# Two layers of linear attention and a squared-ReLU MLP: turned features stored one round later, and one block's normed rows turned by VectorE and reordered through DRAM

## The chip, the cores and the metric

The kernel runs on one core of a Trainium2 chip. The metric is the device time of one execution, in microseconds (us); lower is better. Three runs of the kernel before took 2440.19, 2440.58 and 2441.8 us, median 2440.58. The engines are named as in the profile: PE is the matrix engine (PEld its weight loads), DVE the vector engine, ACT the scalar engine, POOL the GpSimd engine, and SP the queue that issues nearly all DMAs.

## The reference

The input is 2048 rows of 576 features in fp32. Two layers follow each other with the same weights; a layer is linear attention with a learned softmax feature map (32 heads of 18), then an MLP with 4608 hidden units and a squared ReLU, each on layer-normed rows and added to its input.

```python
def _A_ref(x, wqkv, w_phi, wo):          # linear attention
    q, k, v = ...                        # (x @ wqkv), 32 heads of 18
    pq = einsum("bhsd,hdf->bhsf", q, w_phi);  pk = ... the same of k
    phi_q = concatenate([softmax(pq), softmax(-pq)], axis=-1)
    phi_k = concatenate([softmax(pk), softmax(-pk)], axis=-1)
    kv = einsum("bhsf,bhsd->bhfd", phi_k, v);  z = phi_k summed over s
    o = (phi_q @ kv) / (phi_q @ z + 1e-6)
    return o @ wo
def _B_ref(x, w1, b1, w2, b2):           # MLP
    r = maximum(x @ w1 + b1, 0)
    return (r * r) @ w2 + b2
for _ in range(2):
    x = x + _A_ref(layernorm(x), ...)
    x = x + _B_ref(layernorm(x), ...)
```

## The kernel before

**Tiling.** The 2048 rows are four blocks of 512; a block is four tiles of 128 rows. Every fp32 operand of a product is split into a high part (rounded) and a low part (the rest), and a product is made of high x high, high x low and low x high on PE. A block that goes into an MLP must lie turned in SBUF, with the features on the partitions: tiles `...nh` (high, five chunks of 128 x 512) and `...nl` (low, four chunks; the 64 features that remain share the fifth chunk of the high tile, high below and low above).

**Stages of a layer.** First a barrier stage for the block that opens the layer. Then the MLP of that block (in the trace `m_3` in the first layer, `m_1` in the second; here "the first MLP" of a layer), the MLP of a second block (`m_2`, `m_0`; "the second MLP"), and last a stage for the other two blocks together. While an MLP runs, the attention of other blocks is woven into it. In the first layer the first MLP has beside it the output part of the attention of block 2 (tiles `a_2...`) and the queries and feature maps of block 0 (`a_0...`); the second MLP has the output part of block 0 and all of block 1 (`a_1...`). In the second layer the same stages run with other block numbers. In both layers the first woven block is the one that the second MLP then needs.

**The MLP** (`g_mlp`, L1110) runs over 36 chunks f of 128 hidden units. For each, SP loads w1's columns (L1159, L244) and w2's rows (L1161); ACT copies them into high parts (L1167 to L1169), DVE and POOL make the low parts (L1171, L1174, L1175). `hidden` (L1190) makes 14 matmuls into one PSUM tile `ph` (tag "h", a single buffer): 5 of high x high, 4 with the low rows, and 5 with the low weights. `square` lets ACT take the ReLU into `hr` (L1197), its square into `hb` (L1198) and the unrounded square (L1199), and DVE the low part (L1200). `second` makes 15 matmuls into the accumulators `acc` (L1217 and L1208). In the code `second(f - 1)` stands behind `hidden(f)`, so that ACT has a whole chunk's time for the square.

**Weaving.** `weave` (L104) takes a step of the MLP, adds a rate to an account and draws steps of the other generator while the account covers their cost (the number that each `yield` gives). That sets the order of the program; the instruction order on each engine comes from a scheduler that works on it with its own estimates, within the dependences and the `issue_after` bounds. What is left of the other generator at the end of the first MLP is drawn behind the last rows but one of its output ("rows", L1926).

**What the change touches.** `g_features.turn` (L895) turns a tile of 128 rows x 1152 features in 32 x 32 squares on DVE (L897) and stores it with four DMAs into DRAM (`...ft`), in an order that puts features on rows; `g_out.fetch` (L922, L928) loads it back, features on partitions. All DMAs of SP leave in one order, and an issue that waits for its DVE or DMA holds those behind it. `g_out` ends with eight output products of 28 matmuls each (L999, two halves of 288 columns for each of four tiles), their adds on DVE (L1004) and the norm, `g_norm` (L466): statistics on DVE (L459, L462) and POOL (L463, L464), scaling on DVE (L490 and L495), transposes on PE against an identity (L512, 16 of them; L526, 4), and from PSUM the split by ACT (L520, L533) and DVE (L521, L534). `keep` adds a bias on POOL (L1051) and stores the rows (L1052). In `g_attend` (L1680) the cost of each step of this last part is 3.0 where no other norm is given, and its last steps get a cost of 99.0 there, which leaves them to the drain at the end of the MLP; with a norm given they keep their own costs.

## Time and profile before

| | us |
|---|---|
| median of three runs | 2440.58 |
| the profiled execution | 2441.59 |
| its span in the trace | 2439.9 |
| PE busy | 2410.0 (99%) |
| DVE busy | 1560.5 (64%) |
| ACT busy | 1289.7 (53%) |
| POOL busy | 940.6 (39%) |
| first MLP of the first layer, in the trace | 227 to 501.7 |
| second MLP of the first layer | 501.7 to 798.5 |
| first and second MLP of the second layer | 1434 to 1709, 1709 to 2006 |

The profiled execution stands 1.0 us above the median, and 1.7 us of it lie outside the span. A timeline row gives start, duration, engine, line, operation, tiles and shapes, how many instructions in a row it joins, and in brackets the engine's idle time just before and what released it. Matmuls overlap in their records: the distance from one start to the next is what one costs, and that is shorter than its recorded duration. Tile names are joined over blocks and layers of the same name, so a place is given by its time.

### The profile page before, as it was taken

How to read it: one execution, taken by the hardware profiler on the slowest of the kernel's cores; microseconds unless marked ns; L12 is line 12 of the kernel's file. 1: busy time of each engine (PE TensorE's matmuls, PEld its weight loads, DVE VectorE, ACT ScalarE, POOL GpSimd, SP SyncE). 2: the span in 40 equal slices, each digit the busy share in tenths (PEclk: the TensorE clock that was granted, in tenths of full speed). 3: DMA queues.
4: the chain of work that ended last, by engine and by line, in shares of the span. 5: the costliest groups of instructions: out<-in, count | busy, mean ns of one | idle time of the engine just before them, and what ended most of it. 6: DMA issues, size and time to landing. Idle time of an engine off the chain costs nothing. (4 is left out here: it accounts for less than half of the span.)

```text
span 2439.9 us, 41475 instructions
## 1 busy us (share of the span) xinstructions
PE 2410.0 (99%) x14806; PEld 2137.9 (88%) x14806; DVE 1560.5 (64%) x2537; ACT 1289.7 (53%) x2543; POOL 940.6 (39%) x1121
## 2 busy tenths in 40 slices
PE   9999999999999999999999999999999999999999
PEld 8999888888888888888999988888887888888898
DVE  8779847664867655545766787486557675555443
ACT  4344555444456666664443444554455466676643
POOL 4555303212335565542433442032222455565321
PEclk9999999999999999999999999999999999999999
DMA  9124573666654533338753156537667444333364
GB/s 338 64 84 165 163 194 97 151 202 220 155 173 136 157 99 115 109 104 302 257 188 139 59 173 143 168 96 186 191 233 158 141 142 145 118 103 116 110 199 130
DMA packets 370646, 379.40 MB, mean 155 GB/s; under 512 B 142886, under 2 KB 270790, under 8 KB 367878
## 3 DMA queue, kind: packets, MB, share of 16 engines
q1 hardware_dynamic: 369180, 375.37, 51.2%
q8 instruction: 116, 1.90, 0.3%
q10 hardware_dynamic: 1258, 1.37, 0.2%
q14 instruction: 92, 0.75, 0.1%
HBM read 297.22 MB, written 79.41 MB: 154 GB/s over the span
## 5 line engine op out<-in xcount | busy, mean ns | idle before, releaser
L1507 POOL TENSOR_TENSOR m_ps<-m_pr,m_ps 128x128 fp32r<-128x128 f32 x144 | 98.6, 685 | 337.8 <-ACT m_ps L1505 310.7
L1506 DVE TENSOR_TENSOR m_ps<-m_pr,m_ps 128x448 fp32r<-128x448 f32 x144 | 99.8, 693 | 175.9 <-ACT m_ps L1504 175.8
L1549 PE MATMUL m_pacc<-m_ps,m_phb 128*128 128x448 f32 x864 | 185.6, 363 | 0.0
L1549 PEld LDWEIGHTS m_pacc<-m_ps,m_phb 128*128 128x128 f32 x864 | 161.9, 188 | 15.0
L1549 PE MATMUL m_pacacc<-m_ps,m_phc 128*128 128x448 f32 x648 | 147.1, 365 | 0.0
L1504 ACT ACTIVATE m_ps<-m_pr 128x448 fp32r<-128x448 f32 x144 | 82.8, 575 | 115.7 <-issue 64.9
L1549 PEld LDWEIGHTS m_pacacc<-m_ps,m_phc 128*128 128x128 f32 x648 | 119.2, 188 | 7.7
L1190 PE MATMUL m_0ph<-a_0nh,m_0h 128*128 128x512 f32 (+1 forms) x380 | 96.7, 382 | 1.6 <-ACT m_0hr L1197 1.4
L1190 PE MATMUL m_1ph<-t1onh,m_1h 128*128 128x512 f32 (+1 forms) x380 | 96.2, 381 | 2.0 <-ACT m_1hr L1197 1.8
L1217 PE MATMUL m_2acc<-m_2s,m_2hb 128*128 128x448 f32 x432 | 95.2, 367 | 2.9 <-ACT m_2s L1168 2.6
L1190 PE MATMUL m_3ph<-t0onh,m_3h 128*128 128x512 f32 (+1 forms) x380 | 96.1, 381 | 1.8 <-ACT m_3hr L1197 1.6
L1217 PE MATMUL m_0acc<-m_0s,m_0hb 128*128 128x448 f32 x432 | 95.0, 367 | 2.9 <-ACT m_0s L1168 2.6
L1190 PE MATMUL m_2ph<-a_2nh,m_2h 128*128 128x512 f32 (+1 forms) x380 | 96.6, 382 | 0.8 <-ACT m_2hr L1197 0.6
L1217 PE MATMUL m_3acc<-m_3s,m_3hb 128*128 128x448 f32 x432 | 94.2, 364 | 2.0 <-ACT m_3hb L1198 1.4
L1217 PE MATMUL m_1acc<-m_1s,m_1hb 128*128 128x448 f32 x432 | 94.2, 364 | 2.0 <-ACT m_1hb L1198 1.4
L1217 PEld LDWEIGHTS m_2acc<-m_2s,m_2hb 128*128 128x128 f32 x432 | 81.8, 190 | 11.7 <-ACT m_2s L1168 3.0
L1217 PEld LDWEIGHTS m_0acc<-m_0s,m_0hb 128*128 128x128 f32 x432 | 81.5, 190 | 11.7 <-ACT m_0s L1168 3.0
L1217 PEld LDWEIGHTS m_3acc<-m_3s,m_3hb 128*128 128x128 f32 x432 | 80.4, 188 | 10.6 <-ACT m_3hb L1198 2.1
L1217 PEld LDWEIGHTS m_1acc<-m_1s,m_1hb 128*128 128x128 f32 x432 | 80.4, 188 | 10.5 <-ACT m_1hb L1198 2.1
L1175 POOL TENSOR_TENSOR m_3s<-m_3r,m_3s 128x128 fp32r<-128x128 f32 x36 | 22.9, 637 | 161.9 <-ACT m_3s L1169 153.3
L1175 POOL TENSOR_TENSOR m_1s<-m_1r,m_1s 128x128 fp32r<-128x128 f32 x36 | 22.8, 635 | 162.0 <-ACT m_1s L1169 151.8
L1190 PEld LDWEIGHTS m_1ph<-t1onh,m_1h 128*128 128x128 f32 x380 | 68.8, 188 | 17.4 <-ACT m_1hr L1197 3.0
(2464 smaller groups left out, 7237.0 us busy)
## 6 DMA issues: line engine op xcount, KB each, us to landing
m_pr<-in_B_w SPq DMA_DIRECT2D x144, 288.0 KB
m_pr<-in_B_w SPq DMA_DIRECT2D x72, 256.0 KB
hd<-m_pu SPq DMA_DIRECT2D x72, 256.0 KB
m_pg<-hd SPq DMA_DIRECT2D x72, 256.0 KB
m_3r<-in_B_w SPq DMA_DIRECT2D x36, 288.0 KB
m_2r<-in_B_w SPq DMA_DIRECT2D x36, 288.0 KB
m_1r<-in_B_w SPq DMA_DIRECT2D x36, 288.0 KB
m_0r<-in_B_w SPq DMA_DIRECT2D x36, 288.0 KB
```

What stands on the lines that cost most here:

```text
L1175: nc.gpsimd.tensor_sub(s2[:, FC + P : FC + 2 * P], r2[:, R:], s2[:, FC : FC + P].bitcast(F32))
L1190: dense["hidden"] = nc.tensor.matmul(ph[:, cols], a, m, start=(k == 0), stop=(k == len(ops) - 1))
L1217: nc.tensor.matmul(acc[t][:, :R], a[:, rows], m, start=(f == 0 and k == 0), stop=(f == NF - 1 and k == 2))
L1504: nc.scalar.activation(s2[:, RO : RO + R], r2[:, :R], AF.Copy)
L1506: nc.vector.tensor_sub(s2[:, RO + R : RO + 2 * R], r2[:, :R], s2[:, RO : RO + R].bitcast(F32))
L1507: nc.gpsimd.tensor_sub(s2[:, FC + P : FC + 2 * P], r2[:, R:], s2[:, FC : FC + P].bitcast(F32))
L1549: nc.tensor.matmul(accs[b][t][:, :R], a[:, rows], m, start=(g == 0 and k == 0), stop=(g == NF - 1 and k == 2))
```

## The change

Two things are done differently.

First, the stores of the turned features become a stage of their own in the pipeline of `g_features`: tile t is stored one round after it was turned (while the next tile is worked on), and the last one after a further wait of 4.0 cost units. `g_out` waits 3.0 units after its first two fetches.

Second, the norm of the first woven block of each layer is `g_norm_far` in place of `g_norm`. The rows are scaled by one DVE instruction of 128 x 576, turned in 32 x 32 squares by DVE, and stored by four DMAs per tile into a DRAM tile `...xt`, in the same way as the features. One load then fetches the block with the features on partitions into the low tile, and two loads fetch the last 64 features; ACT makes the high parts (L624) and DVE subtracts (L625), chunk by chunk. The 20 transposes of that block on PE fall away. Since a norm is now given, the last steps of `g_out` have their own costs, and are not left to the drain. The rates of the two weaves go from 3.7 to 4.4 and from 5.0 to 5.1.

```diff
@@ -584,6 +584,56 @@
                 apart(NT - 1)
                 yield 1.6
 
+    def blocks_out(home, flat, t):
+        for i in range(NQ):
+            at = t * P + 32 * i
+            nc.sync.dma_start(home[:, at : at + 32].rearrange("(j f) r -> f j r", f=32),
+                              flat[32 * i : 32 * i + 32].rearrange("f (j r) -> f j r", r=32))
+
+    def g_norm_far(x_of, dst, name, then=None):
+        home = dram.tile([D, TB], F32, name=f"{name}xt")
+        xns, raw = {}, {}
+
+        def rows(t):
+            x = x_of(t)
+            mv, rstd = moments(x, t, name)
+            xns[t] = sb.tile([P, D], F32, tag="qk", name=f"{name}n{t}", bufs=5)
+            nc.vector.tensor_scalar(xns[t], x, mv[:, 0:1], rstd, op0=ALU.subtract, op1=ALU.mult)
+            if then:
+                then(t, x)
+
+        def turn(t):
+            nc.vector.transpose(xns[t], xns[t])
+
+        def store(t):
+            blocks_out(home, xns.pop(t), t)
+
+        def land():
+            dst.update(xt_tiles(name))
+            nc.sync.dma_start(dst["l"].bitcast(F32), home[: KC * P].rearrange("(c p) n -> p c n", p=P))
+            raw["t"] = sb.tile([P, TB], F32, tag="ft", name=f"{name}t", bufs=4)
+            load_twice(raw["t"], home, 0, TB)
+
+        def split(c):
+            if c < KC:
+                hi, src, p = dst["h"][:, c], dst["l"][:, c].bitcast(F32), slice(0, P)
+                lo = dst["l"][:, c]
+            else:
+                hi, src, p = dst["h"][:, c], raw["t"], slice(DT, P)
+                lo = dst["h"][DT:, c]
+            nc.scalar.activation(hi, src, AF.Copy)
+            dense["normed"] = nc.vector.tensor_sub(lo, src[p], hi[p].bitcast(F32))
+
+        yield from pipeline(NT, (rows, turn, lambda t: t < NT - 1 and store(t)), (3.0, 0.9, 0.2))
+        yield 3.0
+        store(NT - 1)
+        yield 3.0
+        land()
+        yield 4.0
+        for c in range(NC):
+            split(c)
+            yield 0.8
+
     def spill(b, x):
         nc.sync.dma_start(xth[b], x["h"].rearrange("p c n -> p (c n)").bitcast(F32))
         nc.sync.dma_start(xtl[b], x["l"].rearrange("p c n -> p (c n)").bitcast(F32))
@@ -895,13 +945,18 @@
         def turn(t):
             flat = ph[t].rearrange("p s d -> p (s d)")
             nc.vector.transpose(flat, flat)
-            for i in range(NQ):
-                at = t * P + 32 * i
-                nc.sync.dma_start(home[:, at : at + 32].rearrange("(j f) r -> f j r", f=32),
-                                  flat[32 * i : 32 * i + 32].rearrange("f (j r) -> f j r", r=32))
-
-        yield from held(pipeline(NT, (start, lambda t: soft_exp(ph[t]), add, factors, lambda t: phi_scale(ph[t], rs[t]),
-                                      turn), (2.6, 0.4, 3.0, 2.8, 1.2, 1.6)), ("last", "squared"))
+
+        def store(t):
+            blocks_out(home, ph[t].rearrange("p s d -> p (s d)"), t)
+
+        def steps():
+            yield from pipeline(NT, (start, lambda t: soft_exp(ph[t]), add, factors, lambda t: phi_scale(ph[t], rs[t]),
+                                     turn, lambda t: t < NT - 1 and store(t)), (2.6, 0.4, 3.0, 2.8, 1.2, 1.6, 0.2))
+            yield 4.0
+            store(NT - 1)
+            yield 0.2
+
+        yield from held(steps(), ("last", "squared"))
 
     def g_out(layer, b, ph, dst, name, parts=1, pause=None, behind=None, norm=None, mid=None, costs=(None, None), o_first=None):
 
@@ -1013,6 +1068,7 @@
         if parts == 1:
             for k in range(2):
                 fetch(k)
+            yield 3.0
         xs_of = []
         if pause:
             product, total, factors, rescale = pause
@@ -1839,7 +1895,7 @@
         def back_first():
             m, later = f"a{layer}_{order[2]}", []
             mid = (g_queries(layer, order[2], None, later, m), g_features(layer, later, early, m))
-            yield from g_attend(layer, order[1], None, raws, nxt, f"a{layer}_{order[1]}", dense, None, mid)
+            yield from g_attend(layer, order[1], None, raws, nxt, f"a{layer}_{order[1]}", dense, g_norm_far, mid)
 
         def back_second():
             yield from g_attend(layer, order[2], None, None, operands, f"a{layer}_{order[2]}", None,
@@ -1923,14 +1979,14 @@
                 if last:
                     keep.update(x=xk, es=es, v=wpair("v", f"w{m}"))
 
-        weave(g_mlp(layer, order[0], ready, [], f"m{layer}_{order[0]}", dense.pop("rest")), chained(back_first()), 3.7, "rows")
+        weave(g_mlp(layer, order[0], ready, [], f"m{layer}_{order[0]}", dense.pop("rest")), chained(back_first()), 4.4, "rows")
         back = chained(back_second())
 
         def then():
             drain(back)
             next(products)
 
-        weave(g_mlp(layer, order[1], nxt, [], f"m{layer}_{order[1]}", None, then), back, 5.0)
+        weave(g_mlp(layer, order[1], nxt, [], f"m{layer}_{order[1]}", None, then), back, 5.1)
         back = iter(()) if layer else chained(back_keys(), True)
         for k, _ in enumerate(products):
             if k == NP - 1:
```

What moves on the engines is shown at three places, in the first layer; the second layer has the same. Line numbers behind the change are those of the changed kernel (`hidden` is L1246 there, `second` L1273 and L1264, the copies L1223 to L1225, the low parts L1227 and L1230, the square L1253 to L1256, the stores L590).

On PE, near the end of the first MLP, before: `m_3ph` is the hidden product, `m_3acc` the second one; the number in `m_3h_34` or `m_3s_33` is the chunk f.

```order
L1190 MATMUL m_3ph_5827<-t0onh,m_3h_34_5819 128x512 x5
L1190 MATMUL m_3ph_5827<-t0onl,m_3h_34_5819 128x512 x4
L1190 MATMUL m_3ph_5827<-t0onh,m_3h_34_5819 128x512 x5
L1217 MATMUL m_3acc_3539<-m_3s_33_5655,m_3hb_5843 128x448 x2
L1217 MATMUL m_3acc_3540<-m_3s_33_5655,m_3hb_5843 128x448 x2
L1217 MATMUL m_3acc_3541<-m_3s_33_5655,m_3hb_5843 128x448 x2
L1217 MATMUL m_3acc_3542<-m_3s_33_5655,m_3hb_5843 128x448 x2
```

The same place in the changed kernel:

```order
L1246 MATMUL m_3ph_5865<-t0onh,m_3h_34_5857 128x512 x5
L1246 MATMUL m_3ph_5865<-t0onl,m_3h_34_5857 128x512 x4
L1246 MATMUL m_3ph_5865<-t0onh,m_3h_34_5857 128x512 x5
L1273 MATMUL m_3acc_3539<-m_3s_34_5858,m_3hb_5935 128x448 x2
L1273 MATMUL m_3acc_3540<-m_3s_34_5858,m_3hb_5935 128x448 x2
L1273 MATMUL m_3acc_3541<-m_3s_34_5858,m_3hb_5935 128x448 x2
L1273 MATMUL m_3acc_3542<-m_3s_34_5858,m_3hb_5935 128x448 x2
```

Before, the second product of chunk 33 stands behind the hidden product of chunk 34; now it is that of chunk 34 itself. In the whole first MLP the second product stands directly behind the hidden product of its own chunk at f = 13 before, and at f = 11, 12, 31, 32, 33, 34 and 35 in the changed kernel. There the eight output products of the woven block (112 matmuls `a_2po`) stand in one piece between chunks 28 and 29; before, they were spread from chunk 29 to the end.

On DVE, around the output part of the woven block, before (`a_2x` is a tile of its rows, `a_2nn` and `a_2ne` the normed rows, `m_3h_31` the low weights of chunk 31):

```order
L459 BN_STATS a_2ns_5732<-a_2x_5698 128x6
L462 BN_AGGR a_2nm_5733<-a_2ns_5732 128x2
L490 TENSOR_SCALAR a_2nn_5740<-a_2x_5698,a_2nm_5733,a_2nd_5734 128x512
L1174 TENSOR_TENSOR m_3s_30_5436<-m_3r_30_5430,m_3s_30_5436 128x448
L495 TENSOR_SCALAR a_2ne<-a_2x_5698,a_2nm_5733,a_2nd_5734 128x128
L1171 TENSOR_TENSOR m_3h_31_5494<-m_3r_31_5488,m_3h_31_5494 128x640
```

The end of the same part in the changed kernel:

```order
L1059 TENSOR_TENSOR a_2x_5800<-a_2po_5802,a_2x_5800 128x288
L459 BN_STATS a_2ns_5834<-a_2x_5800 128x6
L1059 TENSOR_TENSOR a_2x_5800<-a_2po_5818,a_2x_5800 128x288
L459 BN_STATS a_2ns_5834<-a_2x_5800 128x6
L462 BN_AGGR a_2nm_5835<-a_2ns_5834 128x2
L601 TENSOR_SCALAR a_2nn_5842<-a_2x_5800,a_2nm_5835,a_2nd_5836 128x576
L606 STREAM_TRANSPOSE a_2nn_5842<-a_2nn_5842 128x576
L1227 TENSOR_TENSOR m_3h_29_5402<-m_3r_29_5396,m_3h_29_5402 128x640
```

Before, two tiles' parts stood together, and low weights were made among them; now the 28 instructions of all four tiles stand in one piece, the low weights of chunk 29 behind them.

On SP, in the middle of the second MLP, before (`m_2r_17` is w2's rows of chunk 17, `a_1ft` the DRAM tile of block 1's turned features, `a_1Q1e` the second of its four tiles):

```order
L1159 DMA m_2r_18_7536<-in_B_w 128x4x128
L244 DMA m_2r_18_7536<-in_B_w 64x128 x2
L900 DMA a_1ft<-a_1Q0e 32x36x32 x4
L900 DMA a_1ft<-a_1Q1e 32x36x32 x4
L1161 DMA m_2r_17_7473<-in_B_w 128x576
L900 DMA a_1ft<-a_1Q2e 32x36x32 x4
L1161 DMA m_2r_18_7537<-in_B_w 128x576
```

The same place in the changed kernel:

```order
L1215 DMA m_2r_18_7519<-in_B_w 128x4x128
L244 DMA m_2r_18_7519<-in_B_w 64x128 x2
L590 DMA a_1ft<-a_1Q0e 32x36x32
L1217 DMA m_2r_17_7456<-in_B_w 128x576
L590 DMA a_1ft<-a_1Q0e 32x36x32 x3
L1217 DMA m_2r_18_7520<-in_B_w 128x576
L590 DMA a_1ft<-a_1Q1e 32x36x32 x4
```

The load of w2's rows for chunk 17 stood behind the stores of two tiles, and stands behind one store of the first; that for chunk 18 stood behind three tiles, and stands behind one.

## The prediction

> **What bounds the kernel now.** I read the page's busy line first, then the busy time by stretch (columns: stretch, length, PE, PEld, DVE, ACT, POOL with their counts, clock, DMA share, GB/s), then what PE waits for.
>
> ```profile
> PE 2410.0 (99%) x14806; PEld 2137.9 (88%) x14806; DVE 1560.5 (64%) x2537; ACT 1289.7 (53%) x2543; POOL 940.6 (39%) x1121
> 230.00:501.70 271.70, 267.97 (x1341) 233.24 (x1339) 187.84 (x279) 140.29 (x257) 74.09 (x76) 1.00 0.60 159
> 501.70:798.50 296.80, 292.51 (x1507) 255.72 (x1505) 191.06 (x315) 156.40 (x308) 99.60 (x124) 0.99 0.60 174
> 1437.00:1709.00 272.00, 268.00 (x1340) 233.00 (x1339) 188.84 (x279) 140.25 (x257) 73.89 (x76) 1.00 0.59 159
> 1709.00:2006.00 297.00, 291.47 (x1503) 255.25 (x1501) 189.84 (x313) 155.35 (x305) 97.98 (x123) 0.99 0.60 174
> ```
>
> PE is busy 99% of the span at full clock, and in the four MLP stretches that the change touches it idles 3.7, 4.3, 4.0 and 5.5 us. So the time is PE's instructions plus PE's waits; work on DVE, ACT or SP counts only where PE waits for it. The waits of PE (total us, times, longest), two rows from the first MLP, two from the second, and the second layer's largest:
>
> ```profile
> PE m_3ph L1190 <- ACT m_3hr L1197: 1.6, 2, 0.8
> PE m_3acc L1217 <- ACT m_3hb L1198: 1.4, 1, 1.4
> PE m_2acc L1217 <- ACT m_2s L1168: 2.6, 1, 2.6
> PE m_2ph L1190 <- ACT m_2hr L1197: 0.6, 1, 0.6
> PE m_0acc L1217 <- ACT m_0s L1168: 2.6, 1, 2.6
> ```
>
> The 1.4 in the first MLP is the one chunk (f = 13) whose second product stands directly behind its own hidden product. The 2.6 in the second MLP is a late copy of weights.
>
> **Term 1: second products directly behind their own hidden product.** The changed order has seven of them in each first MLP, the old one has one. The trace shows its price, first that chunk, then an ordinary one:
>
> ```profile
> 317.57 1.29 PE L1190 MATMUL m_3ph<-t0onh,m_3h 128*128 128x512 f32 x5
> 318.91 0.69 ACT L1197 ACTIVATE m_3hr<-m_3ph,b1t 128x512 f32<-128x512 f32 x1 [6.16 <-PE m_3ph L1190]
> 319.62 0.63 ACT L1198 ACTIVATE m_3hb<-m_3hr 128x512 fp32r<-128x512 f32 x1
> 320.31 2.68 PE L1217 MATMUL m_3acc<-m_3s,m_3hb 128*128 128x448 f32 x12 [1.44 <-ACT m_3hb L1198]
> 323.52 1.30 PE L1190 MATMUL m_3ph<-t0onh,m_3h 128*128 128x512 f32 x5
> ...
> 429.98 1.29 PE L1190 MATMUL m_3ph<-t0onh,m_3h 128*128 128x512 f32 x5
> 431.11 2.57 PE L1217 MATMUL m_3acc<-m_3s,m_3hb 128*128 128x448 f32 x12
> 434.22 1.31 PE L1190 MATMUL m_3ph<-t0onh,m_3h 128*128 128x512 f32 x5
> ```
>
> From the last five hidden matmuls to the next chunk's first: 323.52 - 317.57 = 5.95 us in the direct case, 434.22 - 429.98 = 4.24 in the ordinary one. The difference, 1.71 us, is ACT's ReLU and square (0.69 + 0.63) with the handovers, and nothing of PE's lies behind it. Six more: 6 x 1.71 = **+10.3 us** a layer. ACT started 0.05 us after PE's end there, so it can't be less by an idler ACT. If other ACT work stood between, it would be more.
>
> **Term 2: the eight output products in one piece.** Before, the DVE chain of a tile and the parts of the transpose:
>
> ```profile
> 448.66 1.38 DVE L897 STREAM_TRANSPOSE a_0Q3e<-a_0Q3e 128x1152 f32<-128x1152 f32 x1
> 449.96 0.42 DVE L1004 TENSOR_TENSOR a_2x<-a_2po,a_2x 128x288 f32<-128x288 f32 x1
> 452.97 0.55 DVE L490 TENSOR_SCALAR a_2nn<-a_2x,a_2nm,a_2nd 128x512 f32<-128x512 f32 x1 [1.00 <-POOL a_2nd L464]
> 453.69 0.45 DVE L1004 TENSOR_TENSOR a_2x<-a_2po,a_2x 128x288 f32<-128x288 f32 x1
> 458.12 0.81 DVE L1171 TENSOR_TENSOR m_3h<-m_3r,m_3h 128x640 fp32r<-128x640 f32 x1
> ```
>
> A tile takes 453.69 - 449.96 = 3.73 us, with PE's products back to back beside it. In the changed order a tile takes 3.01 us to the scaling (449.96 to 452.97), about 0.62 for 576 columns (scaled from 0.55 for 512) and half of 1.38 for its transpose: 4.3 us, and four of them 17.2, while PE needs 4 x 3.73 = 14.9. The chain starts one product (1.9 us) after PE and ends at 19.1; behind it stands the low part of chunk 29's weights (0.81), at 19.9. PE, which has two PSUM tiles for these products, is held up about 1 us among them, and then gets 2.0 us into chunk 29 (nine matmuls) before it needs those low weights, so it waits 2 to 3 us more: about 4 in all. Of the old order's waits in this place one is a 0.8 for the ReLU, where two hidden products stand together; such a pair stands in both orders and stays. What else can go is what PE's idle time in the stretch (3.7 us) leaves beside the 1.6 and 1.4 of the wait rows: 0.7, with its handovers some 1 us. I take 4 - 1 = **+3.0** a layer, between 0 (if DVE keeps pace with PE) and +4.2 (if none of the old waits go).
>
> **Term 3: the end of the first MLP.**
>
> ```profile
> 500.30 1.14 DVE L1275 TENSOR_TENSOR m_3x<-m_3acc,m_3x 128x448 f32<-128x448 f32 x2
> 501.73 0.84 PE L1190 MATMUL m_2ph<-a_2nh,m_2h 128*128 128x256 f32 x5
> 502.63 0.67 DVE L1277 TENSOR_TENSOR m_3x<-m_3py,m_3x 128x128 f32<-128x128 f32 x3
> 497.56 0.60 ACT L520 ACTIVATE a_2nh<-a_2np 128x512 fp32r<-128x512 f32 x1 [4.84 <-PE a_2np L512]
> ```
>
> In the changed order ACT makes one high part of the landed rows (0.60) between the last chunk's ReLU and its square, which that chunk's direct product waits for: +0.6. DVE's eight adds for the output rows (four of 0.57 and four of 0.22, 3.2 us) and a low part (0.81) now stand ahead of the new MLP's first low weights; PE has four transposes and 16 half-width matmuls at 0.13 or so to do meanwhile, some 2.7 us: +1.1 to +1.3. I take **+1.7** a layer, between 0 and +4.0 (all of DVE's work uncovered).
>
> **Term 4: 20 transposes leave PE.**
>
> ```profile
> L512 PE MATMUL a_2np<-ident,a_2nn 128*128 128x128 f32 x16 | 2.4, 272 | 0.0
> 454.26 0.60 PE L512 MATMUL a_2np<-ident,a_2nn 128*128 128x128 f32 x4
> 455.05 0.40 PE L999 MATMUL a_2po<-a_2o0h,a_2oh 126*128 126x288 f32 x1 [0.18 <-DVE a_2x L1004]
> 496.92 0.60 PE L512 MATMUL a_2np<-ident,a_2nn 128*128 128x128 f32 x4
> 497.28 1.17 PE L1208 MATMUL m_3acc<-m_3hb,m_3s 128*128 128x512 f32 x4
> ```
>
> Each is recorded with 272 ns, but four of them move what follows by 0.36 us (496.92 to 497.28), or 0.61 less the wait (454.26 to 455.05). At 0.4 for four: **-2.0** a layer, between -1.8 and -3.1. [...]
>
> **Term 5: the late weights in the second MLP.**
>
> ```profile
> SPq L900 <- DVE a_1Q1e L897: 7.9, 1, 7.9
> 649.43 2.33 SPq L900 DMA_DIRECT2D a_1ft<-a_1Q1e  x4
> 651.86 0.59 SPq L1161 DMA_DIRECT2D m_2r<-in_B_w  x1
> 655.61 1.29 PE L1190 MATMUL m_2ph<-a_2nh,m_2h 128*128 128x512 f32 x5
> 658.86 0.56 ACT L1168 ACTIVATE m_2s<-m_2r 128x448 fp32r<-128x448 f32 x1
> 664.63 2.57 PE L1217 MATMUL m_2acc<-m_2s,m_2hb 128*128 128x448 f32 x12
> ```
>
> The first row is SP's wait, the others are instructions. w2's rows for chunk 17 leave SP behind the stores of block 1's second tile, which waited 7.9 us for its transpose; ACT's copy of them stands behind chunk 18's ReLU and squares and starts at 658.86. Chunk 17's second product takes from 656.74 (655.61 plus 1.13, as 429.98 to 431.11) to 664.63, 7.89 us where an ordinary one takes 434.22 - 431.11 = 3.11: 4.8 us lost. Changed, that load stands behind one store of the first tile, and the copy ahead of chunk 18's ReLU: the loss goes. Late next is the first load for chunk 19, now behind the third tile's stores, and one more pair of hidden products (chunks 19 and 20) at the 0.8 of the wait rows: together about +1, against about 0.7 of smaller waits that go. I take **-4.5** a layer, between 0 (the stall only moves) and -7.2 (all of PE's waits here go).
>
> **Costed at nothing.** The added stores (16 a layer, of 128-byte runs), the three loads and DVE's four transposes lie beside PE; the DMA share is 0.60 in these stretches. SP has the loads for the block ahead of the end: it issues them behind those of chunk 35's weights, which wait for chunk 33's to be used, some two chunks (2 x 8.0 us) before ACT copies the block. If that cover is gone, each us is a us on PE, since the last square stands behind a copy.
>
> **The sum.** +10.3 + 3.0 + 1.7 - 2.0 - 4.5 = +8.5 a layer, +17.0 for both. Against the profiled execution that is 2441.6 + 17.0 = 2458.6; it stands 1.0 above the median of the runs, so I predict a median of **2457.6**.
>
> **The rivals.** (a) *The waits are made up again* (other side, faster). If something other than PE set the pace of the first MLP, the weights' arrival say, PE would run into the same later waits sooner or later, and terms 1 to 3 (15.0 us) would vanish in them: -2.0 - 4.5 = -6.5 a layer, 2427.6. It turns the sign once less than 6.5 / 15.0 = 43% of the waits is charged. Against it: PE is busy 268.0 of 271.7 us there, and the chunk behind the direct one ran on at full pace.
>
> (b) *Gains and losses nearly cancel.* All 7.2 us of PE's waits in the second MLP go, and terms 2 and 3 are 0: 10.3 - 2.0 - 7.2 = +1.1 a layer, 2442.8.
>
> (c) *The change doesn't free the weights.* Stores of a tile still wait in SP ahead of weights, and if the first store of the first tile or chunk 19's load waits as long as before, term 5 is 0: +13.0 a layer, 2466.6. For it: SP waited 7.9 us for a transpose here, and DVE is no quicker.
>
> (d) *The rows land late.* Price: each us beyond the cover of 16 us, in both layers; 5 us too late gives 2457.6 + 10 = 2467.6. Stores of this form land quickly in the trace:
>
> ```profile
> 658.25 3.26 SPq L900 DMA_DIRECT2D a_1ft<-a_1Q3e  x4
> 664.30 0.80 SPq L928 DMA_DIRECT2D a_1w<-a_1ft  x2
> ```
>
> The fetch that reads all four tiles' stores left SP 2.8 us after the last store. [...]
>
> **Chances.** My forecast 0.60 (2447 to 2464 on its own terms), (a) 0.09, (b) 0.13, (c) 0.13, (d) 0.05. A measurement of this kernel can tell about 0.2% (4.9 us) from no change; so faster 0.09, same 0.13, slower 0.78. The range takes in (b) and (c) and leaves out (a), longer forms of (d) and all far ends at once: 2441 to 2468.
>
> **What would show it.** In the profile after, the wait of the second product for ACT's square (L1254 there) should be seven times in each first MLP, about 10 us in total, and each first MLP about 13 us longer; a wait for the low weights of chunk 29 of 2 to 3 us behind the eight products; no PE wait for the copy of w2's rows in the second MLPs, each about 4.5 us shorter. If the direct products show waits but the first MLPs are no longer, (a) is right; if the second MLPs are as long as before, (c); if ACT waits for the landed block's load, (d). The forecast is wrong if the waits for the square are well under 1.4 us each.

## The result and the profile after

The changed kernel takes 2477.86 us (median of four runs, 2474.92 to 2481.13); the kernel before took 2440.67 (median of four, three of them the runs named above). The ratio is 1.0152, with a 95% interval of 1.0134 to 1.0170: slower, as forecast, but by 37 us where 17 were forecast, and outside the range. The profiled span grew from 2439.9 to 2478.3 us, by 38.4. First the page's busy line, then the four MLP stretches by windows (columns as in the prediction: stretch, length, PE, PEld, DVE, ACT, POOL with counts, clock, DMA share, GB/s; the third row begins 2.0 us behind the start of its MLP and the fourth ends 3.0 us ahead of its end):

```profile
PE 2420.4 (98%) x14766; PEld 2140.3 (86%) x14766; DVE 1559.3 (63%) x2535; ACT 1291.7 (52%) x2541; POOL 946.6 (38%) x1121
230.40:519.30 288.90, 272.59 (x1321) 234.13 (x1319) 185.61 (x274) 139.35 (x253) 77.57 (x75) 0.98 0.56 148
519.30:815.80 296.50, 292.20 (x1508) 254.74 (x1507) 194.11 (x318) 158.59 (x311) 98.71 (x123) 1.00 0.64 184
1459.00:1748.00 289.00, 272.60 (x1328) 234.46 (x1327) 186.22 (x277) 139.48 (x253) 78.60 (x76) 0.98 0.56 149
1748.00:2039.40 291.40, 288.85 (x1494) 252.39 (x1493) 191.42 (x314) 155.35 (x304) 96.59 (x120) 1.00 0.64 185
```

PE has 40 instructions fewer, yet is busy 10.4 us longer: the clock column of the first MLPs points at the reason, 0.98 where it was 1.00. PE's idle time grew by 28.0 us. The waits of PE over 2 us behind the start of the program, and two smaller ones (total us, times, longest); where both layers have the same wait, the first layer's row stands here:

```profile
PE m_3acc L1273 <- ACT m_3hb L1254: 8.6, 6, 1.4
PE m_3acc L1264 <- ACT m_3hb L1254: 1.8, 1, 1.8
PE m_3ph L1246 <- DVE m_3h L1227: 3.6, 1, 3.6
PE m_ppx L1573 <- DVE m_pu L1705: 4.5, 2, 2.2
PE kvp L753 <- issue: 3.2, 1, 3.2
PE m_2ph L1246 <- ACT m_2h L1223: 2.1, 2, 1.3
PE m_2ph L1246 <- ACT m_2hr L1253: 0.9, 1, 0.9
```

The seven direct second products wait (8.6 + 1.8), the low weights of chunk 29 wait 3.6, and no second product waits for a copy of w2's rows any more. The rows of `m_pu` and `kvp` stand in stages that the change doesn't touch. By stage (from PE's first hidden product of one MLP to that of the next; the pair stage of the first layer holds the second layer's barrier):

| stage | before | after | difference | forecast |
|---|---|---|---|---|
| start to the first MLP | 227.1 | 227.5 | +0.4 | 0 |
| first MLPs, layer 1 / 2 | 274.6 / 275.1 | 291.8 / 291.0 | +17.2 / +15.9 | +13.0 each |
| second MLPs | 297.1 / 298.4 | 296.5 / 294.4 | -0.6 / -4.0 | -4.5 each |
| pair stage and barrier | 635.2 | 641.2 | +6.0 | 0 |
| last pair stage | 432.4 | 435.9 | +3.5 | 0 |
| sum | 2439.9 | 2478.3 | +38.4 | +17.0 |

Of the 21.4 us that the sum lacked, 7.1 lie in the first MLPs, 4.4 in the second, 9.5 in the pair stages and 0.4 at the start. The first part is read from PE's rows behind chunk 29's wait, and the clock there and at the end of that MLP:

```profile
461.75 2.50 PE L1246 MATMUL m_3ph<-t0onh,m_3h 128*128 128x512 f32 x5 [3.61 <-DVE m_3h L1227]
465.03 2.50 PE L1246 MATMUL m_3ph<-t0onh,m_3h 128*128 128x512 f32 x5 [0.78 <-ACT m_3hr L1253]
467.33 1.91 PE L1246 MATMUL m_3ph<-t0onl,m_3h 128*128 128x512 f32 x4
470.83 2.57 PE L1273 MATMUL m_3acc<-m_3s,m_3hb 128*128 128x448 f32 x12
461.70:470.80 9.10, 8.27 (x19) 6.04 (x20) 3.02 (x4) 1.95 (x3) 1.11 (x2) 0.52 0.68 167
515.00:521.00 6.00, 6.00 (x29) 5.31 (x29) 5.50 (x12) 4.72 (x11) 0.46 (x1) 0.73 0.00 1
```

Five hidden matmuls take 2.50 us in place of 1.3, at a clock of 0.52: this wait is paid twice, once as idle time and once more as slow matmuls behind it.

### The profile page after: what moved, and what is told of

It reads as the page before. It is cut to its first block, busy times and chain, and to the rows that moved or that the text cites. A ratio compares the mean times of both kernels' runs of the same rounds, so it can differ in the third digit from the quotient of the medians.

```text
span 2478.3 us, 41486 instructions
## 1 busy us (share of the span) xinstructions
PE 2420.4 (98%) x14766; PEld 2140.3 (86%) x14766; DVE 1559.3 (63%) x2535; ACT 1291.7 (52%) x2541; POOL 946.6 (38%) x1121
## 4 chain that ended last, share of the span: by engine, by line
PE 87%; DVE 6%; DMA 2%; ACT 2%; issue 1%; POOL 1%; SPq 1%; DVEq 0%; ACTq 0%; POOLq 0%
PE m_ppx L1573 9%; PE m_pacc L1605 7%; PE m_pacacc L1605 5%; PE m_3ph L1246 5%; PE m_1ph L1246 4%; PE m_ppy L1573 4%; PE m_0ph L1246 4%; PE m_3acc L1273 3%; PE m_1acc L1273 3%; PE m_2ph L1246 3%; PE m_0acc L1273 3%; PE m_ppz L1573 2%; PE m_2acc L1273 2%; PE m_pacc L1595 2%; PE m_pacacc L1595 2%; PE m_pach L1605 2%
## 5 line engine op out<-in xcount | busy, mean ns | idle before, releaser
L1246 PE MATMUL m_3ph<-t0onh,m_3h 128*128 128x512 f32 (+1 forms) x380 | 99.2, 390 | 5.4 <-DVE m_3h L1227 3.6
L1273 PE MATMUL m_1acc<-m_1s,m_1hb 128*128 128x448 f32 x432 | 95.3, 369 | 8.8 <-ACT m_1hb L1254 8.6
L1273 PE MATMUL m_3acc<-m_3s,m_3hb 128*128 128x448 f32 x432 | 95.4, 368 | 8.7 <-ACT m_3hb L1254 8.6
L1246 PE MATMUL m_1ph<-t1onh,m_1h 128*128 128x512 f32 (+1 forms) x380 | 98.5, 388 | 5.4 <-DVE m_1h L1227 3.6
L1246 PE MATMUL m_2ph<-a_2nh,m_2h 128*128 128x512 f32 (+1 forms) x380 | 97.4, 384 | 3.5 <-ACT m_2h L1223 2.1
L1246 PE MATMUL m_0ph<-a_0nh,m_0h 128*128 128x512 f32 (+1 forms) x380 | 97.3, 384 | 2.5 <-ACT m_0hr L1253 1.4
L1273 PEld LDWEIGHTS m_1acc<-m_1s,m_1hb 128*128 128x128 f32 x432 | 81.5, 190 | 19.5 <-ACT m_1hb L1254 11.2
L1273 PEld LDWEIGHTS m_3acc<-m_3s,m_3hb 128*128 128x128 f32 x432 | 81.4, 190 | 19.5 <-ACT m_3hb L1254 11.2
L1273 PE MATMUL m_0acc<-m_0s,m_0hb 128*128 128x448 f32 x432 | 93.9, 363 | 0.0
L1273 PE MATMUL m_2acc<-m_2s,m_2hb 128*128 128x448 f32 x432 | 93.9, 363 | 0.0
L1246 PEld LDWEIGHTS m_3ph<-t0onh,m_3h 128*128 128x128 f32 x380 | 70.6, 193 | 21.8 <-DVE m_3h L1227 4.0
L1246 PEld LDWEIGHTS m_1ph<-t1onh,m_1h 128*128 128x128 f32 x380 | 70.0, 192 | 21.6 <-DVE m_1h L1227 4.2
L1273 PEld LDWEIGHTS m_0acc<-m_0s,m_0hb 128*128 128x128 f32 x432 | 80.8, 188 | 7.9 <-ACT m_0hb L1254 0.2
L1273 PEld LDWEIGHTS m_2acc<-m_2s,m_2hb 128*128 128x128 f32 x432 | 80.8, 188 | 7.9 <-ACT m_2hb L1254 0.2
```

The lines of the kernel that those rows point to most:

```text
L1246: dense["hidden"] = nc.tensor.matmul(ph[:, cols], a, m, start=(k == 0), stop=(k == len(ops) - 1))
L1273: nc.tensor.matmul(acc[t][:, :R], a[:, rows], m, start=(f == 0 and k == 0), stop=(f == NF - 1 and k == 2))
```

## The experiments

Times are medians of 4 to 11 runs where nothing else is said; the ratio is to the kernel before on the same chip. The diffs name the lines that count.

**Which half costs.** The new norm alone, with each tile stored as it is turned, the first rate at 4.4 and the second back at 5.0:

```diff
-                                     turn, lambda t: t < NT - 1 and store(t)), (2.6, 0.4, 3.0, 2.8, 1.2, 1.6, 0.2))
-            yield 4.0
-            store(NT - 1)
-            yield 0.2
+                                     lambda t: (turn(t), store(t))), (2.6, 0.4, 3.0, 2.8, 1.2, 1.6))
...
-            yield 3.0
```

> The other part alone: the norm turned on VectorE with its rate of 4.4, the stores as before, rate 5.0. PE's order has four direct second products per first MLP (11, 30, 31, 32), 112 output products in two pieces around chunk 26. Theory: 3 x 1.7 for directs, a wait behind the output products of about 3 with a stretch at half clock (about 4), less 2 for the transposes, 10 a layer, plus 3 to 4 once for the instruction wait at the second layer's barrier: near 2464; second MLPs as before, with the stall of chunk 17's weights. Rival (most of the loss is from the stores): near 2445.

Measured 2481.03 (1.0162, 1.0147 to 1.0178): above both forecasts, with first MLPs of 290.3 and 289.1. This half alone brings a loss as large as the whole change. The other half alone, with the old norm and the old rates 3.7 and 5.0:

```diff
-            yield from g_attend(layer, order[1], None, raws, nxt, f"a{layer}_{order[1]}", dense, g_norm_far, mid)
+            yield from g_attend(layer, order[1], None, raws, nxt, f"a{layer}_{order[1]}", dense, None, mid)
```

> One part of the change alone: the stores one round later, with the kernel before's norm on PE and its rates. PE's order has two direct second products per second MLP (chunks 19 and 20) and two instead of one per first MLP (chunks 13 and 35); 34 of the last output products stand past the end of the first MLP. Theory: the 4.8 us stall of chunk 17's weights goes in each second MLP, the directs give back 2 x 1.7 there and 1.7 in the first, and a late prelude costs the pair stages about 2: near 2443, same as before. Rival (the stores are the part that costs): near 2455 or more.

Measured 2481.19 (1.0167, 1.0145 to 1.0190), a miss: the second MLPs took 313.1 and 311.6. With the old rates the added cost units pushed output work out of the first MLPs, so that run mixes two things. Without the added units (the last line is the wait behind the first fetches in `g_out`):

```diff
-                                     turn, lambda t: t < NT - 1 and store(t)), (2.6, 0.4, 3.0, 2.8, 1.2, 1.6, 0.2))
-            yield 4.0
+                                     turn, lambda t: t < NT - 1 and store(t)), (2.6, 0.4, 3.0, 2.8, 1.2, 1.4, 0.2))
             store(NT - 1)
-            yield 0.2
+            yield 0.01
...
-            yield 3.0
```

> The kernel before with the first half of the change alone: the turned features are stored one round later, but the extra stage has no cost (the turn 1.4 and the store 0.2 in place of the turn's 1.6, and none of the waits of 4.0 and 3.0 units), with the old norm and the old rates. If the 16 and 13 us that the second MLPs lost in the earlier run of this half came from the added cost units, which pushed the output part past the end, the second MLPs come back to 293 to 298 us here and the time to 2438 to 2446. The stall of chunk 17's weights (2.6) goes, and chunk 19's first load, now behind the stores of two tiles, waits 3 to 4 us instead. If the stores themselves, issued one round later, cost the time (SP's queue held, weights late), the second MLPs stay above 305 us and the time above 2465.

Measured 2441.24 (0.9998, 0.9989 to 1.0006), second MLPs 295.7 and 299.0: the cost units were the cause, and the half itself gains nothing. The 2.6 us stall of chunk 17 is gone and a wait of 2.2 for chunk 19 stands in its place (in the second layer one of 2.3 for chunk 20's ReLU beside it).

**The direct products.** In the changed kernel, `second(f - 1)` is bound behind `hidden(f)`:

```diff
-            second(f - 1)
+            with tc.issue_after(dense["hidden"].ins):
+                second(f - 1)
```

> The changed kernel, but the second product of a chunk is bound behind the hidden product of the next chunk, so that no second product stands directly behind its own hidden product (seven in each first MLP now). Theory: each costs 1.7 us of PE waiting for ACT's ReLU and square, so 7 x 1.7 = 12 us a layer go, about 24 in all: near 2454. The eight output products in one piece and the long wait behind them stay. Rival (the arrival of weights sets the pace and PE meets the same waits elsewhere): no gain, near 2478.

Measured 2460.03 (1.0075, 1.0058 to 1.0092). The first MLPs fall by 16.2 and 17.0 us (to 275.6 and 274.0), so the waits of the direct products were real and nothing made them up. But the second MLPs grow by 6.6 and 4.2, since PE now waits for weights there (first row; the second is chunk 29's wait in the first MLP, which stays):

```profile
PE m_2ph L1246 <- ACT m_2h L1223: 7.9, 3, 4.5
PE m_3ph L1246 <- DVE m_3h L1227: 3.6, 1, 3.6
```

**The eight products in one piece.** The rows of a tile wait for the low weights of the chunk before, which spreads the products over four places:

```diff
         def rows(t):
-            x = x_of(t)
-            mv, rstd = moments(x, t, name)
+            with tc.issue_after(dense["low"].ins):
+                x = x_of(t)
+                mv, rstd = moments(x, t, name)
```

> The changed kernel, but each tile's add and norm chain on DVE is bound behind the low weights of the latest chunk, which spreads the eight output products over four chunks (28 matmuls each). Five of the seven direct second products stay (f = 11, 12, 33, 34, 35). Theory: the wait of 3.6 us for the low weights of chunk 29 goes, and with it the halved clock seen behind it (granted clock 0.52 for 9 us, some 4 us lost), about 1 us of waits among the products and two direct products (3.4 us): some 12 us a layer, near 2454. Rival (the slow stretch has nothing to do with the wait): only 3.6 + 1 + 3.4 = 8 us a layer go, near 2462, and the granted clock still drops near chunk 30.

Measured 2461.7 (1.0081, 1.0065 to 1.0097): first MLPs 282.4 and 281.1, some 10 us less each. That is the rival's time, but the rival did not happen: chunk 29's wait is gone and the clock does not drop at chunk 30. In its place PE waits 3.07 us (first layer) and 3.21 us (second) for later weights, and only the first of the two is followed by half the clock (0.73 granted from 490 to 495; 1.00 from 1710 to 1720, around the second). Both edits together:

> Both bounds together: no direct second product, output products spread. Theory: 12 + 8.6 = about 20 us a layer go, near 2437, and no stretch of the first MLPs is below a granted clock of 1.0. Rival (weights set the pace): above 2465.

Measured 2463.68 (1.0092, 1.0077 to 1.0107), far from the sum of the two gains and near the rival's time: first MLPs 277.1 and 277.6. A third wait, for weights, had taken over. In the stretch 440 to 520 of that run, PE's and SP's waits:

```profile
PE m_3ph L1249 <- ACT m_3h L1224: 6.8, 3, 5.7
SPq L1109 <- POOL a_2x L1108: 25.5, 4, 7.6
```

SP's store of the finished rows stands ahead of the next weights and waits for POOL's bias add. A first try moved `keep` whole to the store's round:

> The kernel with the turned rows, the products spread in four pieces and no direct second products, and beside that the bias add on POOL and the store of the rows moved one step on, from the scaling to the store of the turned rows. If what kept the first MLP at 277 us in that kernel was SP's queue, held by row stores that waited 25 us in all for POOL's adds, with the weights behind them, that wait falls below 8 us, the first MLPs come to 270 to 273 us and the time to 2448 to 2454. If the weights were late for another reason (the landing, the DMA load), the first MLPs stay at 276 to 278 and the time at 2458 to 2464.

Measured 2465.53 (1.0100, 1.0084 to 1.0115), first MLPs 275.5 and 276.2. The edit moved POOL's add along with the store, and SP still waited 21.2 us in three places there, so that run says nothing for or against the queue. Then the store alone (`then` is `keep`, called here without its add):

```diff
-            if then:
-                then(t, x)
+            xs[t] = x
+            nc.gpsimd.tensor_add(x, x, b2t)
...
         def store(t):
             blocks_out(home, xns.pop(t), t)
+            then(t, xs.pop(t), False)
```

> The kernel with the turned rows, the products in four pieces and no direct second products; the bias add on POOL stays at the scaling, but the store of the rows alone moves one round on, beside the store of the turned rows. In the last such run the add moved along with the store, so SP waited for it as long as before. If SP's queue, held by row stores that wait for POOL, is what makes the weights of chunks 31 to 34 late, SP's wait for POOL falls from 21 to 25 us to below 5 there, PE's wait for the first weights (5.7 and 4.6 us before) goes below 2 us, the first MLPs come to 270 to 273 us and the time to 2448 to 2456. If the weights are late for another reason, the first MLPs stay at 275 to 278 and the time at 2460 to 2466.

Measured 2448.65 (1.0029, 1.0017 to 1.0041): SP's wait for POOL is gone there (it still waits 17.1 us, for DVE to turn the normed rows), PE waits 0.2 us in all, and the first MLPs take 267.8 and 267.6, 7 us less than in the kernel before. The row stores in SP's queue were the cause. The turned rows are a part of that gain: with the old norm and no direct products (a run further down) the first MLPs take 271.1 and 270.6, so some 3 of the 7 us. The second MLPs, 306.6 and 303.0, take it back.

**The clock.** Does a wait cost more than its length? In the kernel before, the ReLU of two chunks of each second MLP is made 8 and 10 times (first layer), 9 and 13 times (second), with the same result, so that PE waits for it:

```diff
-            nc.scalar.activation(hr, ph, AF.Relu, bias=b1t[:, f : f + 1])
+            for _ in range(repeats.get((name, f), 1)):
+                nc.scalar.activation(hr, ph, AF.Relu, bias=b1t[:, f : f + 1])
```

> The kernel before with ACT's ReLU of four chunks in the second MLPs made 8, 10, 9 and 13 times over (first layer chunks 12 and 15, second layer chunks 12 and 15; same result), so that PE waits for the hidden tile about 0.69 us times the count less 3.1: 2.4, 3.8, 3.1 and 5.9 us, 15 in all. PE's order is unchanged. Theory (a wait of PE beyond some 3 us halves its granted clock for several us): behind the waits of 3.8 and 5.9, and perhaps 3.1, the granted clock falls to about half for up to 9 us, costing some 4 us each; time 2464 to 2468. Rival (waits alone): 2456, granted clock 1.0 throughout.

Measured 2465.43 in one run. The four waits were 3.7 to 7.5 us, 20.9 in all and not 15, so that the time falls into the forecast by luck. The rows carry the result: the 14 hidden matmuls behind a wait, usually 3.2 us, took 1.6 to 2.4 us more each time. Then made 5, 4, 6 and 7 times:

> The kernel before with the ReLU of four chunks repeated 4, 5, 6 and 7 times, where it was 8, 9, 10 and 13 times: by the fit of the earlier run (wait = 0.71 x repeats - 1.96 us) PE waits about 0.9, 1.6, 2.3 and 3.0 us there, 7.8 us in all. If only a wait beyond some 3 us is followed by a stretch at half the clock, the time is 2441.6 + 7.8 = 2449 to 2451, and the five matmuls behind each wait take their usual 1.3 us but for the last. If any wait of 1 us or more does it, each adds 1.7 us more, 2456, and the five take 2.5.

Measured 2449.53 in one run. The time alone would speak for the first case, but the rows show half the clock behind shorter waits than 3 us too (granted 0.66 in the 4.5 us behind the second row's wait, 0.57 in the 4.0 behind the third's):

```profile
623.96 1.43 PE L1192 MATMUL m_2ph<-a_2nh,m_2h 128*128 128x512 f32 x5 [1.56 <-ACT m_2hr L1200]
1833.52 2.50 PE L1192 MATMUL m_0ph<-a_0nh,m_0h 128*128 128x512 f32 x5 [2.28 <-ACT m_0hr L1200]
1857.08 2.50 PE L1192 MATMUL m_0ph<-a_0nh,m_0h 128*128 128x512 f32 x5 [3.00 <-ACT m_0hr L1200]
```

Last, the changed kernel with chunk 29's wait filled: its first nine matmuls are made once more ahead of all fourteen:

```diff
+            if (name, f) in (("m0_3", 29), ("m1_1", 29)):
+                for k, (a, m) in enumerate(ops):
+                    nc.tensor.matmul(ph[:, cols], a, m, start=(k == 0), stop=(k == len(ops) - 1))
```

> The changed kernel, with the first nine hidden matmuls of chunk 29 made twice (the second time from a fresh start, so that the sums stay the same); they stand in front of the wait for that chunk's low weights, which is 3.6 us in each first MLP, and take some 2.0 us of it. The low weights come when they came, so by waits alone nothing changes: 2475 to 2481. If the half clock behind a wait of over some 2.3 us is what this wait costs beside its length, the 1.5 us that are left of it leave the clock at 1.00, the matmuls of chunks 29 and 30 take their usual 1.3 us for five, and each first MLP is 3.5 to 4.5 us shorter: 2468 to 2471.

Measured 2472.1 (1.0123, 1.0109 to 1.0137), 5.8 us below the changed kernel with 18 matmuls more, and between the two forecasts. The time doesn't decide, since the wait at the barrier (taken up next) happens to be gone as well, 3.5 us (that stage 641.2 to 637.7). PE's rows of the profiled run, the fastest of the four (2467.91), first layer, then second:

```profile
461.60 1.43 PE L1249 MATMUL m_3ph<-t0onh,m_3h 128*128 128x512 f32 x5 [1.56 <-DVE m_3h L1227]
463.81 1.41 PE L1249 MATMUL m_3ph<-t0onh,m_3h 128*128 128x512 f32 x5 [0.78 <-ACT m_3hr L1256]
467.10 2.57 PE L1276 MATMUL m_3acc<-m_3s,m_3hb 128*128 128x448 f32 x12
...
1682.02 1.43 PE L1249 MATMUL m_1ph<-t1onh,m_1h 128*128 128x512 f32 x5 [1.55 <-DVE m_1h L1227]
1684.22 2.50 PE L1249 MATMUL m_1ph<-t1onh,m_1h 128*128 128x512 f32 x5 [0.78 <-ACT m_1hr L1256]
1688.93 2.56 PE L1276 MATMUL m_1acc<-m_1s,m_1hb 128*128 128x448 f32 x12
```

The low weights came at the same time (461.60, before 461.75), and the next second product starts 5.50 us later in place of 9.08: 3.6 us of clock in the first layer. In the second layer the clock stays through the 1.55 and falls behind the next wait of 0.78, so part of the loss is still there. The first MLPs are 4.9 and 2.4 us shorter; 1.4 us of each come from their end, where the same wait of 1.81 us halved the clock in the changed kernel and left it alone here, which was not forecast. By waits alone nothing would have changed.

**The two waits in the pair stages.** 20 transposes that nobody reads are put at the program's start, to shift PE's instructions:

```diff
+    padded = wtile("padded")
+    for i in range(20):
+        nc.tensor.transpose(padded[:, i % 4 * P : (i % 4 + 1) * P], ident, ident)
```

> The changed kernel with 20 dummy transposes of the identity at the very start, where PE is idle for 4 us, so that PE's program before the second layer's barrier is as long again as in the kernel before. Theory: the wait of 3.2 us there, in the middle of 64 like matmuls and put down to issue, is PE's instructions arriving late behind 2 MB of loads, and whether a refill falls into these loads hangs on how many instructions PE has had; with the padding it falls back to 0.6 us or less and the stage from the end of the second MLP to the next first MLP gets about 3 to 4 us shorter: near 2474. Rival (it comes from something else in the changed kernel): the wait stays, 2478.

Measured 2477.72 (1.0147, 1.0132 to 1.0162): the rival's time, but not its mechanism: the wait at the barrier is gone (that stage 641.2 to 638.2), and 3.8 us are lost at the start. The second rate from 5.1 to 5.6:

> The changed kernel with the second weave's rate at 5.6 in place of 5.1, which brings the pair stage's first weights about two chunks earlier in ACT's and SP's order. Theory: the 2.2 us that PE waits in each pair stage for a DVE sum that stands behind late weights go: about 4.5 less, near 2473; one direct second product (chunk 18) more or less in the second MLPs. Rival (the wait has another cause): unchanged.

Measured 2486.25 (1.0185, 1.0168 to 1.0202), above both forecasts: the two waits for `m_pu` are gone (last stage 435.9 to 432.0), and the second MLPs lose 5.4 and 7.3.

**The second MLPs.** The free later stores (the third run above) with the bound of `second(f - 1)`:

> The run with stores one round later at no cost, with every second product bound behind the next chunk's hidden products, so that no second product stands directly behind its own hidden ones. If each direct product of the old order costs the 1.4 to 1.7 us of its wait and nothing makes it up, this is 2 to 7 us faster than that run: 2432 to 2440. If the bound only moves the waits to weights and ReLU, as it did in the second MLPs of the changed kernel, the time stays within 2440 to 2450.

Measured 2440.55 (0.9999, 0.9990 to 1.0007), the second case. The first MLPs gain 4.0 and 4.5 us against that run (271.1, 270.6), and the second lose 4.9 and 1.3 (300.6, 300.3), with waits of 5.3 and 6.4 for chunk 19's weights. Is it SP's queue or the DMA engines? Each store is bound behind the newest load:

```diff
         def store(t):
-            blocks_out(home, ph[t].rearrange("p s d -> p (s d)"), t)
+            with tc.issue_after(dense["load"].ins):
+                blocks_out(home, ph[t].rearrange("p s d -> p (s d)"), t)
```

> The kernel before with stores one round later at no cost and no direct second products, where the second MLPs waited 5.3 and 6.4 us for chunk 19's weights behind two tiles' stores; now each store of turned features is bound behind the loads of the weights of the chunk that is current in the program, so that these leave SP first. If the stores ahead of the loads in SP's queue are the cause, that wait falls below 2 us, the half clock behind it goes, the second MLPs come to 292 to 296 us and the time to 2424 to 2432. If the loads are late because the DMA engines are busy (share 0.96 to 1.24 around that place), the wait stays at 4 us or more and the time at 2436 to 2444.

Measured 2440.48 (0.9996, 0.9987 to 1.0004), wait 5.7. The bound did not reach chunk 19's load, which still left behind two tiles' stores, so that says nothing about the question. The same bound in the kernel with the store apart gave 2447.62 (1.0021, 1.0012 to 1.0030; 2440 to 2447 was expected), with second MLPs of 300.0 and 305.7, and says as little. Then the stores of the third and fourth tile are kept back until the next chunk's loads are issued:

```diff
+            if t >= 2 and "load" in dense:
+                postponed.append(out)
...
             dense["load"] = nc.sync.dma_start(r2, w2[cols])
+            flush()
```

> The run with stores one round later at no cost and no direct second products, as it was tried with the bound behind the loads; but there chunk 19's load still left SP behind the stores of the third and fourth tile, and its wait stayed (5.7 us). Here the stores of those two tiles are kept back until the next chunk's loads are issued, so that chunk 19's first load stands ahead of them and leaves some 8 us earlier (about 650 us in the place of 658). If SP's queue is the cause, PE's wait for it (5.3 and 5.7 us, with half clock behind) goes, the second MLPs come to 292 to 296 us and the time to 2424 to 2432. If the busy DMA engines are the cause (share 1.19 in the 5 us ahead of the wait), a wait of 3 us or more stays and the time is 2434 to 2441.

Measured 2445.02 (1.0019, 1.0010 to 1.0028), neither forecast. Without this edit (the free later stores with the bound of `second(f - 1)`), and then with it, SP's issue of chunk 19's load and ACT's copy of it, and the waits that are left:

```profile
657.91 0.64 SPq L1213 DMA_DIRECT2D m_2r<-in_B_w  x1
661.98 0.74 ACT L1221 ACTIVATE m_2h<-m_2r 128x640 fp32r<-128x640 f32 x1 [5.30 <-DMA m_2r<-in_B_w]
```

```profile
652.39 1.76 SPq L1226 DMA_DIRECT2D m_2r<-in_B_w  x1
659.43 0.73 ACT L1235 ACTIVATE m_2h<-m_2r 128x640 fp32r<-128x640 f32 x1
669.12 0.96 PE L1258 MATMUL m_2ph<-a_2nh,m_2h 128*128 128x512 f32 x3 [2.34 <-ACT m_2h L1235]
671.86 0.79 PE L1031 MATMUL a_1pn<-a_1fh,kbh 126*126 126x512 f32 x1 [1.77 <-ACT a_1fh L1008]
```

The load left 5.5 us earlier and ACT no longer waited for it: the place in the queue was the cause of that wait. But the next chunk waits 2.34 and the features, whose stores are now later, 1.77: the wait moved on. In the first MLPs the same edit cost 3.6 and 5.4 us. The same, from the second tile on, in the kernel with the store apart:

> The kernel with the turned rows, the row stores apart, four pieces of products and no direct second products, where the second MLPs took 306.6 and 303.0 us; here the stores of the second to fourth tile of turned features are kept back until the next chunk's loads are issued, so that the loads of chunks 19 and 20 stand ahead of them in SP's queue. If the queue is the cause, PE's waits for the first weights there (9.2 and 6.0 us in three places each) fall below 3 us in all, the second MLPs come to 295 to 299 us and the time to 2430 to 2438, under the kernel before. If not, the second MLPs stay above 301 us and the time at 2443 to 2450.

Measured 2457.89 (1.0068, 1.0054 to 1.0082), above both forecasts. The second MLPs are as expected, 295.2 and 294.0: from chunk 11 on PE has no wait of 0.5 us or more in either. The first ones are 12.8 and 11.0 us longer than without the edit, with a new wait of 7.0 for weights and half the clock behind it (five hidden matmuls in 2.50 us). The two good halves (first MLPs of the one run, second of the other) would add up to a span of some 2428 us (2448.4 - 11.4 - 9.0, by their stage times), 12 below the kernel before; keeping stores back in the second MLPs alone was not run, so that is an estimate.

## Why the prediction was right in direction and short in size

**The step that failed** stands ahead of the terms: "So the time is PE's instructions plus PE's waits". It takes PE's instructions to last what they lasted before, so that a wait costs its length and no more. The runs show that a wait can halve the clock for what follows (0.52 in the 9.1 us behind chunk 29's 3.61), and that this was the largest part of what the first MLPs lacked. The second failure is in term 5, and the third is that the pair stages were put at nothing.

**Term 1 (direct products, +10.3 a layer)** holds: waits of 8.6 + 1.8 against 1.4, 9.0 us more before handovers. Rival (a) falls for them: with those waits taken away, the first MLPs got 16 us shorter. What (a) names does happen once the products are spread as well: then a wait for weights took back part of the two gains, until the row stores were moved.

**Terms 2 and 3 (+3.0 and +1.7)** priced the waits about right. Chunk 29's wait was 3.6 (said 2 to 3) and those among the products 0.6 (said 1); at the end it was 0.9 in place of 1.7 (0.5 behind the new MLP's start, and 1.81 for 1.44 at the last direct product). What was missing is the clock. From the end of chunk 29's wait to the next second product it took 9.08 us in the first layer and 8.25 in the second, where 5.50 are enough at full clock (the run with the wait filled): 3.6 and 2.75 us more. The end of the MLP cost 1.4 us more in each layer. Together that is 5.0 and 4.1, where 4.2 and 2.9 were lacking, so the other terms were about 1 us too high together. The kernel before had shown it, in the rows that term 5 was taken from:

```profile
659.47 0.49 PE L1217 MATMUL m_2acc<-m_2s,m_2hb 128*128 128x448 f32 x1 [2.57 <-ACT m_2s L1168]
660.26 3.83 PE L1217 MATMUL m_2acc<-m_2s,m_2hb 128*128 128x448 f32 x11 [0.30 <-DVE m_2s L1174]
660.00:665.00 5.00, 4.74 (x16) 4.23 (x17) 0.83 (x2) 0.78 (x2) 1.22 (x2) 0.68 1.24 210
```

The loss of 4.8 us was split nowhere in the prediction: 2.9 are wait, and the eleven matmuls that follow take 3.83 where twelve take 2.57. Whoever asks why 4.8 is more than 2.6 has the missing term. The prediction's own window rows give the clock as 0.99 in both second MLPs, beside its sentence "at full clock".

**Term 4 (-2.0)** holds. Two runs have next to no waits in their first MLPs, one with the transposes (stores later, no direct products) and one without (the store apart). PE is busy there for 269.7 and 269.8 us in the one, and for 267.5 and 267.2 in the other: 2.2 and 2.6 less.

**Term 5 (-4.5)** came out at -0.6 in the first layer and -4.0 in the second, and in the run of that half alone at -1.4 and +0.6. The stall of chunk 17's weights did go, with the slow matmuls behind it. The step that failed is "late next is the first load for chunk 19 ... together about +1". In the first layer PE idles 4.3 us in the second MLP before and after: in the stall's place stand waits of 0.8 (chunk 4), 0.7 (a query product beside chunk 10), 1.3 (chunk 19) and 0.9 (chunk 20). In the second layer its idle time falls from 5.5 to 2.5 us. So one layer was nearly right and the other wrong. The 7.2 of the lower bound and of rival (b) has no row of its own: the idle time with some 1.9 us of slow matmuls is 6.2 and 7.4.

Is DVE the limit, on whose turns the stores wait? It is full ahead of the stall, before and after, but it is just as full in the last run, where the second MLPs have no stall (third row):

```profile
640.00:655.00 15.00, 15.00 (x71) 12.91 (x70) 14.76 (x24) 5.78 (x10) 4.94 (x4) 1.00 0.58 98
645.00:660.00 15.00, 15.00 (x71) 13.12 (x70) 14.86 (x20) 9.41 (x17) 7.27 (x6) 1.00 0.34 96
645.00:660.00 15.00, 15.00 (x70) 12.90 (x69) 14.88 (x22) 8.01 (x15) 6.14 (x6) 1.00 0.51 108
```

DVE works 14.76, 14.86 and 14.88 of 15.00 us. So a full DVE alone does not make the stall. What the runs show is that the order of stores and loads in SP's queue decides which chunk pays: 17 before, 19 and 20 after, 20 with two tiles' stores kept back, and none with three. Rival (c) spoke of that queue, with a chance of 0.13, and its sign ("the second MLPs are as long as before") came in the first layer only; with it alone the sum would have been 2466.6, still 11 short. Rival (d) falls: the block landed early, and ACT made its first high part 18.6 us after the load left SP, without a wait:

```profile
494.36 0.38 SPq L613 DMA_DIRECT2D a_2nl<-a_2nxt  x1
513.00 0.62 ACT L624 ACTIVATE a_2nh<-a_2nl 128x512 fp32r<-128x512 f32 x1
```

**What no term had** are 9.5 us in the pair stages. At the barrier PE stands still for 3.2 us in the middle of 64 like matmuls, for nothing that the profile shows ("issue"); in the pair stages PE waits twice 2.2 for a sum on DVE that stands behind a low part of late weights:

```profile
1405.46 0.32 PE L753 MATMUL kvp<-k_lastK3e,vs 128*32 128x36 f32 x12
1408.98 1.01 PE L753 MATMUL kvp<-k_lastK3e,vs 128*32 128x36 f32 x52 [3.19 <-issue]
829.45 0.42 DVE L1529 TENSOR_TENSOR m_pwa<-m_pr,m_pwa 128x256 fp32r<-128x256 f32 x1 [2.82 <-ACT m_pwa L1528]
830.59 0.73 PE L1573 MATMUL m_ppx<-a_1nt4h,m_pwb 128*128 128x512 f32 x2 [2.24 <-DVE m_pu L1705]
```

The first shows in every run with the changed kernel's PE count (14766), with 2.9 to 4.1 us, and in none with the old one, and goes when 20 instructions are put ahead: it hangs on the number of PE's instructions ahead of it. Whether it is the fetch of instructions, held by loads, was not shown. The second goes with another rate; why the order of the changed kernel brings it is open. Of the remaining 1.8 us, 1.6 are the clock once more: behind the second wait for `m_pu` the same matmuls took 6.40 us (2057.20 to 2063.60), where they took 4.82 behind the first (830.59 to 835.41).

## What to carry to other kernels

A wait of the matrix engine can cost more than its length: here the slow matmuls behind it came to 1.4 to 3.6 us. The next section shows when: the same idle time is cheaper in pieces of up to 1.4 us, well apart, than in one. A stall that sits behind a queue's order can be moved by reordering, and once it went altogether, but the same edit cost the first MLPs 11 to 13 us, so try such an order stage by stage. In a queue that leaves in one order, a store that waits for a slow engine delays the loads behind it (four row stores waited 25.5 us for POOL here, and PE then 6.8 for weights); issuing it one round later, without the work it waits for, gained 9 us in each first MLP here (277.1 to 267.8).
